# Batch 4's input product in block form at the end of a fused attention and MoE kernel, and the order of all later work set anew

## The chip, the cores and the metric

The kernel runs on one core of a Trainium2 chip. The metric is the device time of one execution in microseconds. The engines are named as the profile names them: PE is TensorE's matmul, PEld its weight load, DVE is VectorE, ACT is ScalarE, POOL is GpSimd, SP is SyncE. L12 is line 12 of the kernel before.

## The reference

For 8 batches of 12 heads with 448 rows of 64, an attention without softmax gives x, and x goes through a feed-forward layer of 768 to 2048 to 768:

```python
scores = scale * np.matmul(q, k.transpose(0, 1, 3, 2))
attn = np.maximum(scores, 0.0) ** 2 / S
x = np.matmul(attn, v)            # heads put side by side: 3584 x 768
h = x @ w_in                      # 768 -> 2048
g = 0.5 * h * (1.0 + erf(h * inv_sqrt2))
return (g @ w_out).astype(np.float32)
```

## The kernel before

**Attention of a batch** is 21 steps in three groups of 7. A step is 4 small matmuls (QK, L742), a relu from PSUM to SBUF on ACT (L754) or DVE (L756), and a square on DVE (L763). After 7 steps 28 small matmuls (AV, L803) make a third of x, which two casts bring to SBUF (L516 on DVE, L518 on ACT).

**The input product** (`x @ w_in`) has two forms. The plain one, `add_f1`, makes 16 column blocks of a batch, each of 6 matmuls of 128x448 (L855), and one gelu on ACT (L865) for each. The block form, `add_blocks`, is a 2x2 block product with 7 products in place of 8 (Winograd's form): four sums of x on DVE (L966), then in four parts (m4 and y), each with 7 products of 6 matmuls of 128x224 (L999), one copy on ACT (L518), five additions on DVE (L1036) and four gelus on ACT (L1045). The parts of one m4 run side by side in the two banks of a PSUM tile. The names of a part are p1, p6, p2, p7, p5, p4, p3 for products; v1 is the copy behind p1, v2 the addition behind p6, v3 that behind p7, c22, c21 and c12 those behind p5, p4 and p3. p2 waits for v1, p7 for v2, p4 for v3 and p3 for c22. Sums of the weights for this form are made once (`add_wsums`, 8 operations, L924). Before the change batches 5, 6 and 7 take the block form; batches 0 to 4 take the plain one.

**The output product** (`g @ w_out`) runs in 13 groups of 256 rows (`add_group`, g1 to g13), again 7 products of 8 matmuls of 128x384 (L1173), with four sums on DVE (L1154) and seven additions or copies, most of them on DVE (L1207); group 0 is plain (L1268). A group's first 128 rows (x=0) and last 128 rows (x=1) are stored from SBUF tiles called osb, of which there are three. The last group, g13, stores in four pieces: the left half of its first rows; all of its last rows; and the right half of the first rows in 256 and 128 columns, behind two additions that follow the two parts of its last product. One piece of each of these last two goes out on ACT's queue, all other stores on SP's.

**Loads** of q, k and v go through POOL's queue. From batch 2 on, q and k are turned by DMA transposes on SP's queue (L665). The swap of halves that follows is two DMAs on SP (L686, L687) or two copies on DVE (L516). The next batch's loads wait for the turned data (gates on POOL, L710).

**The order of all work** is a list, ORDER (L86). A word is an engine letter (P, A, D, G, S) and the number of the operation as the code creates it. `place` commits the words in turn, and `run` emits the operations in that sequence. So for each engine and each queue the list is the program order, and an instruction that waits holds up what follows on its own engine or queue. The planner's costs, due times and readers are consulted for the words' sense; they issue nothing.

Of the kernel before, what the change touches and what calls it, by code (L numbers as in the profile page):

```python
# [9 lines left out]
BF16 = mybir.dt.bfloat16  # L10
# [6 lines left out]
HS = S // 2  # L17
# [69 lines left out]
G0 G1 G3 G4 G1428 G7 G121 A10 P11 D13 G2 A16 P17 D12 P14 G117 D18 P42 P39 G6 P21 D15 P19 A43 G118  # L87
P36 D22 P33 A40 P23 G5 D20 P25 D41 P54 A37 G122 D24 Z1056 D26 A34 P66 P57 D38 A55 D44 G8 P63 P29
P27 A58 D67 P69 P51 D35 A64 P48 D30 P31 D65 A70 P45 D28 D32 A52 P78 D59 G9 P133 D46 A49 P108 D68
D47 P111 A79 P75 D134 P129 A109 D50 P81 P131 D56 A76 P102 D112 P84 G125 A82 D71 P72 D53 A103 G120  # L90
P60 D130 A85 D104 P93 A73 P135 A61 D110 A74 A62 P96 D132 P105 G124 P141 D83 D77 A97 P168 A94 D106
P165 P90 A142 G119 P143 D86 D113 A169 G126 D107 P114 A166 D80 P87 D98 A91 D95 P171 A144 D115 P137
A88 D92 A116 P99 D89 P156 A172 D136 P159 A100 D138 P145 G128 A157 A101 D160 P162 P186 D167 P174
A146 P251 D163 A175 P243 D158 A187 D176 G148 A252 D170 P183 P195 P189 G147 D173 A244 P259 G151
A196 D184 G154 P253 D161 A260 G150 D164 P139 A190 P198 A254 P180 P177 D140 A181 D199 P219 P216
P245 A178 G123 G127 A220 D217 P207 A179 P210 P204 D191 A246 P261 S229 A211 D208 P247 D182 A205
S228 D209 A262 D197 P213 P222 P192 D200 S232 A248 P263 D221 A223 D206 P249 D224 A264 D188 P255
D212 A250 P257 D193 A214 A256 D194 P265 D218 A258 D185 P201 D230 D215 A266 G237 S231 G239 P225
A202 A203 P276 P279 P267 D233 D226 S235 A277 A227 P291 D280 P288 P294 A268 P356 G240 A295 D289
G153 G238 P350 A357 G149 P348 G270 A292 A351 P285 P300 P303 G272 A349 P354 G241 A301 P364 A304  # L100
A355 P312 P318 P362 A365 P370 D319 D281 A363 D296 P358 A313 D236 D290 A286 P282 P306 A371 P315
P352 A359 D307 P360 A353 P376 A361 P368 A316 A377 D317 P372 D314 A369 D308 P366 D293 A373 P378
A283 A367 D284 P374 S234 A379 D390 P382 D278 S399 A375 D391 D392 P380 D417 D418 D305 G242 G152
D302 D287 G269 S398 P327 P339 D320 P297 G271 D396 G155 A328 D383 P333 G274 P384 D381 G273 D298
A340 A299 D393 A334 D394 P330 P324 P309 D329 P387 D419 A331 D335 A385 S402 A310 D395 D311 S386
A325 P342 P336 S401 P321 D397 D400 D388 A343 D332 P421 A322 D337 A323 P423 D420 D338 D422 S405
P446 P443 D341 P449 P425 D424 D344 A450 S404 S403 S406 P427 G413 D444 G275 A426 G409 S389 D447
P429 D326 D428 P452 P455 P345 A456 D453 P440 P437 D445 P431 D430 A441 D560 P433 D346 A347 D432
S435 P473 A438 P461 P470 D434 S436 P509 G407 G408 G410 A471 D474 P513 D448 G412 A462 S542 D457
A510 G411 P479 D454 P476 P464 G415 A514 P519 D472 D442 G414 A465 D439 P517 A520 D477 P515 A480  # L110
D451 A518 S541 P485 P467 P458 A468 P491 A516 S545 P511 D459 A486 D561 P523 A492 D487 A512 D460
P503 P494 P500 D563 A524 P525 D463 S544 A495 D466 P521 D469 A526 D481 P531 D504 A522 D478 P527
A532 D501 P537 D475 S548 A528 D505 P529 D502 A538 D493 S547 S543 S546 S549 P488 P497 P482 A498
D489 P606 G556 P600 G552 G416 P535 A483 A530 G550 P533 D601 G551 A607 D484 A536 G553 D490 G555
P539 D496 G554 D499 P609 G559 P603 P506 G558 A604 D610 G557 P624 A534 P639 D562 P564 A540 D605
A507 P566 A640 D625 D565 D508 P615 P612 P618 D567 P568 A616 D613 P570 D617 A569 D611 D614 P572
S705 D619 P657 D571 P627 P636 S704 P574 D580 D573 A637 D620 P576 D608 A658 D575 S578 A628 P584
D581 S708 D638 D577 P586 D583 S579 D582 P630 D602 P633 P621 D626 A634 D631 P651 A585 S707 P642
P588 D632 D587 A643 D659 P590 D629 A652 A622 D641 D591 P648 A623 D644 P666 P663 A589 S711 D653
P592 D635 A664 S710 S706 S709 S712 G719 P594 G715 A649 D667 D593 P654 P660 P645 A655 D661 P769  # L120
P763 D595 P596 S598 D725 A770 G713 G714 A646 P672 D764 G716 D597 S599 P674 G718 D665 D650 A673
G717 G721 A647 D656 P772 P778 P775 G720 D662 A675 P678 S868 A776 D779 P676 D668 A773 D771 P766
D777 P787 P669 S867 A767 D788 A679 P781 P790 A677 D774 P682 A670 D723 D768 P684 A782 A671 D724
A683 D765 P680 D783 A791 D780 P796 P799 P784 A681 S871 A800 D797 P793 P802 P688 D803 D804 S870
D798 D789 D792 S874 S873 S869 S872 S875 G882 G722 A785 A685 P686 A794 A689 A786 P811 P823 P805
A687 P690 D795 A806 P692 A691 D824 P698 D726 A812 D807 A693 P696 D801 A699 P814 P817 P808 A697
A815 D818 P820 P906 G878 P694 A809 G876 G877 P702 D907 G879 A695 A810 G881 P700 G880 A821 G884
A703 P826 P829 D822 P912 A701 P727 A827 P729 D828 A728 D813 P731 A913 D730 A830 D816 P733 D819
D825 P921 D831 P909 P832 A910 D922 P918 P936 D732 G885 P735 D734 A833 G883 D911 A919 D834 P924
P915 A937 P737 D736 A916 D925 P930 P933 D938 P942 P739 D743 A931 D738 S741 D744 P747 A934 D745  # L130
D740 S742 P749 D917 A748 D935 S979 P751 D914 A943 D920 D750 S978 P753 D944 A752 D746 S982 P755
D923 D926 D754 P757 D932 D908 P939 P948 P927 D758 S981 A940 D949 P960 P945 D941 P835 A928 D756
D950 A946 P759 A929 S761 D961 S985 D947 P957 P954 P951 A836 D760 S984 S980 S983 S986 A958 D955
P963 P966 P839 D956 A952 S762 D953 A967 P837 D959 A840 P969 D964 P972 P987 A838 D888 P841 A973
P843 D988 D965 A842 D989 P845 A970 D962 A844 D974 P847 D971 A846 D1067 P1002 D968 P990 P975 A1003
D991 A848 P993 P996 P851 D976 A994 A977 P999 D997 P1014 P1005 A852 D1004 P849 D995 D992 P853 D886
A850 D1068 P857 D998 A1000 A854 P855 D1015 A1006 D1001 P1017 D1007 P1026 P1008 D1070 A1027 D1018
P1029 A856 P1011 P859 A858 D1059 A1009 D1028 P863 D1019 A1030 A860 D1031 P865 A1012 D1060 A864
A1010 P1035 D887 P1047 P1020 D1016 A866 P861 A1048 P890 D1021 A1036 A862 D1063 D1022 P1023 P1041
P1044 A891 D1013 P892 A1024 D1042 P1053 A1045 D1025 P1050 P1032 D1069 A1051 D1054 P1038 P1071  # L140
A1033 D1062 P894 D1049 A1072 D1043 P1088 D893 A1039 P1073 A1034 D1066 A895 P1079 A1089 D1040
P1090 D889 P1096 P1075 D1091 P896 D1055 D1074 D1181 P1094 D1052 P1077 D897 P1092 P898 D1095 D1078
P1082 D1064 P1099 P900 D1061 D899 D1097 P902 D1083 D1100 P1105 D1080 D901 S904 P1102 A1076 D1179
P1085 A1106 D1139 P1122 A1093 D1046 A1084 P1107 D1037 P1124 A1123 D903 S905 P1109 A1081 D1086
P1126 D1103 A1087 P1113 D1108 P1130 D1125 A1110 P1128 A1127 D1065 P1111 A1104 D1140 A1098 P1056
D1180 D1129 D1112 P1133 D1131 P1143 D1057 D1114 P1119 D1058 P1136 D1134 D1291 P1116 D1144 P1183
D1120 P1200 D1137 P1185 D1117 P1202 A1184 D1141 A1201 P1191 D1182 P1187 D1203 P1145 D1186 P1189
P1206 P1208 P1147 D1190 D1207 D1146 P1194 D1192 P1211 D1209 P1149 D1195 P1214 D1212 D1148 P1217
D1150 P1197 D1142 P1151 A1218 A1115 D1198 A1118 P1221 D1215 A1135 P1234 D1152 A1121 P1219 A1132
P1236 A1101 A1138 P1153 A1235 D1237 P1238 D1161 P1155 D1220 D1154 S1157 P1240 D1159 P1223 D1156  # L150
S1158 P1163 D1160 D1241 P1245 P1165 D1164 D1224 P1228 P1167 D1166 D1162 D1246 P1169 D1229 D1168
P1225 P1171 D1170 D1253 P1173 D1172 D1226 P1175 D1251 P1242 P1231 A1239 P1204 A1222 P1303 A1227
D1243 P1248 D1176 S1178 A1188 P1320 A1205 D1252 P1295 A1210 D1174 S1177 A1244 D1232 P1312 A1199
D1292 P1255 A1230 D1249 A1296 D1254 A1313 P1297 D1293 A1193 P1314 A1196 P1299 A1256 P1257 A1233
D1298 A1213 D1315 A1216 P1301 P1316 D1258 P1318 P1261 D1319 P1259 D1302 D1304 D1294 P1309 D1262
P1323 A1260 A1250 P1263 D1310 A1247 D1324 P1306 D1321 P1265 D1264 D1307 P1326 P1329 P1346 D1327
P1331 D1271 P1267 A1347 D1272 A1330 P1350 P1348 D1268 S1270 P1333 P1275 D1349 D1266 S1269 D1273
P1277 D1276 P1279 D1274 D1332 D1278 P1352 P1335 A1280 P1281 P1283 D1282 P1285 D1365 D1353 D1336
# [239 lines left out]
def kernel(  # L398
# [738 lines left out]
    def add_group(g):  # L1137
# [116 lines left out]
        for bb in bs:  # L1254
            readers.setdefault(bb, []).extend(mine)
# [287 lines left out]
```

## Time and profile before

| what | value |
|---|---|
| median of the runs | 369.87 us (369.41 to 371.4) |
| the profiled execution | 368.93 us, its span 367.2 us |
| PE busy | 358.1 us, 98% of the span |
| DVE busy | 291.2 us, 79% |
| ACT busy | 191.8 us, 52% |
| POOL busy | 63.5 us, 17% |
| granted TensorE clock | 0.996 |

The profile shows one execution. Its span is from the first to the last instruction; the execution's own time is 1.73 us longer. A group's busy time divided by its count is the time that an instruction takes from the engine in a row of such instructions; the mean of one is longer, since instructions overlap at their ends.

### The profile page before, as it was taken

The page shows a single profiled execution, that of the slowest core. Times are in us where ns is not written, and L with a number is a line of the kernel's source. Part 1 is how long each engine was busy: PE and PEld are TensorE (multiplying, and loading weights), DVE is VectorE, ACT ScalarE, POOL GpSimd, SP SyncE. Part 2 cuts the span into 40 slices and gives each one's busy share as a digit, 9 for nine tenths or more (in the row PEclk, how much of TensorE's full clock was granted, in tenths as well). Part 3 has the DMA queues.
Part 4 walks back from the last instruction along what each step waited for, and adds up shares of the span by engine and source line. Part 5 has one row for each costly group of instructions (what it writes and reads, how often), then busy time and mean ns, then how long its engine had stood idle before and what let it go on. Part 6 is the DMA issues. An engine that isn't in the chain of part 4 may idle for free.

```text
span 367.2 us, 8476 instructions
## 1 busy us (share of the span) xinstructions
PE 358.1 (98%) x3560; PEld 222.3 (61%) x3560; DVE 291.2 (79%) x488; ACT 191.8 (52%) x312; POOL 63.5 (17%) x101
## 2 busy tenths in 40 slices
PE   8889999999999999999999999999999999999994
PEld 7666654455544555544455544478888787867662
DVE  3999882689996899998579999999977766667753
ACT  4987867637377544678665466951414134133100
POOL 8565134410600700501310000000000000000000
PEclk9999999999999999999999999999999999999998
DMA  9999999999999999999949770000200211022233
GB/s 172 200 200 204 188 141 203 191 197 157 162 258 172 185 167 188 175 247 161 190 68 201 142 158 2 2 2 5 83 2 1 87 48 40 14 73 87 86 86 88
DMA packets 74406, 46.19 MB, mean 126 GB/s; under 512 B 38400, under 2 KB 70912, under 8 KB 74368
## 3 DMA queue, kind: packets, MB, share of 16 engines
q0 software_dynamic: 32912, 22.47, 42.2%
q1 hardware_dynamic: 40816, 22.67, 29.5%
q8 instruction: 28, 0.46, 0.5%
q10 hardware_dynamic: 640, 0.51, 0.4%
q14 instruction: 10, 0.08, 0.1%
HBM read 45.61 MB, written 11.01 MB: 154 GB/s over the span
## 4 chain that ended last, share of the span: by engine, by line
PE 95%; ACT 3%; issue 1%; DVE 0%; DVEq 0%
PE pso L1173 33%; PE psh L855 26%; PE pb L999 13%; PE ps L742 10%; PE pav L803 9%; ACT a_sq L754 3%; PE pso L1268 3%; PE spin L1340 1%; PE tp L638 0%; PE tp L610 0%; DVE qT L516 0%; DVEq L1538 0%; DVE osb L1207 0%; DVE zero L1324 0%
## 5 line engine op out<-in xcount | busy, mean ns | idle before, releaser
L754 ACT ACTIVATE a_sq<-ps 128x896 bf16<-128x896 f32 (+1 forms) x116 | 102.5, 923 | 44.1 <-PE ps L742 41.1
L763 DVE TENSOR_TENSOR a_sq<-a_sq 128x896 bf16<-128x896 bf16 x169 | 97.1, 614 | 8.0 <-ACT a_sq L754 7.7
L855 PE MATMUL psh<-xT,win_sb 128*128 128x448 bf16 (+1 forms) x516 | 96.3, 340 | 0.0
L855 PEld LDWEIGHTS <-win_sb 128*128 128x128 bf16 x516 | 47.9, 98 | 45.9 <-issue 9.8
L756 DVE TENSOR_SCALAR a_sq<-ps 128x896 bf16<-128x896 f32 (+1 forms) x53 | 57.0, 1078 | 16.6 <-PE ps L742 16.4
L1173 PEld LDWEIGHTS <-s_sb 128*128 128x128 bf16 x424 | 40.7, 98 | 25.7 <-issue 1.8
L865 ACT ACTIVATE h_sb<-psh 128x448 bf16<-128x448 f32 x80 | 43.5, 550 | 22.3 <-PE psh L855 22.0
L742 PE MATMUL ps<-qT,kT 64*64 64x448 bf16 (+1 forms) x756 | 47.9, 336 | 1.0 <-ACT a_sq L754 0.4
L1036 DVE TENSOR_TENSOR part<-pb,part 128x448 f32<-128x448 f32 x60 | 35.2, 617 | 13.6 <-PE pb L999 11.5
L1173 PEld LDWEIGHTS <-h_sb 128*128 128x128 bf16 x312 | 29.8, 98 | 20.9 <-issue 3.2
L1173 PE MATMUL pso<-wout_sb,h_sb 128*128 128x384 bf16 x208 | 38.1, 326 | 0.0
L1173 PE MATMUL pso<-wout_sb,s_sb 128*128 128x384 bf16 (+2 forms) x216 | 38.1, 320 | 0.0
L1173 PE MATMUL pso<-t_sb,s_sb 128*128 128x384 bf16 x208 | 38.1, 326 | 0.0
L803 PE MATMUL pav<-a_sq,v_sb 64*64 64x448 bf16 (+1 forms) x756 | 36.3, 329 | 1.3 <-issue 1.1
L1207 DVE TENSOR_TENSOR osb<-pso,p_sb 128x384 f32<-128x384 f32 x39 | 21.5, 551 | 13.0 <-PE pso L1173 11.2
L742 PEld LDWEIGHTS <-kT 64*64 64x64 bf16 x756 | 18.6, 105 | 21.1 <-issue 16.2
L999 PEld LDWEIGHTS <-win_sb 128*128 128x128 bf16 x288 | 27.5, 98 | 2.9 <-issue 0.7
L803 PEld LDWEIGHTS <-v_sb 64*64 64x64 bf16 x756 | 21.1, 107 | 13.0 <-issue 2.3
L1045 ACT ACTIVATE h_sb<-part 128x448 bf16<-128x448 f32 x36 | 18.4, 576 | 19.0 <-DVE part L1036 18.9
L710 POOL COPY gate<-qT 128x16 bf16<-128x16 bf16 x15 | 5.2, 345 | 100.2 <-DMA qT<-nq 79.9
L518 ACT CAST xT<-pav 128x448 bf16<-128x448 f32 (+1 forms) x38 | 18.3, 500 | 7.7 <-PE pav L803 6.3
L999 PEld LDWEIGHTS <-ws 128*128 128x128 bf16 x216 | 20.8, 98 | 1.2
(58 smaller groups left out, 300.5 us busy)
## 6 DMA issues: line engine op xcount, KB each, us to landing
nk<-in_k_dram POOLq DMA_DIRECT2D x23, 224.0 KB, 10.3
nq<-in_q_dram POOLq DMA_DIRECT2D x21, 224.0 KB, 10.2
v_sb<-in_v_dram POOLq DMA_DIRECT2D x5, 672.0 KB, 9.1
qT<-qT SPq DMA_DIRECT2D x28, 112.0 KB, 2.6
out_dram<-osb SPq DMA_DIRECT2D x8, 336.0 KB, 3.0
v_sb<-in_v_dram POOLq DMA_DIRECT2D x9, 224.0 KB, 9.4
out_dram<-osb SPq DMA_DIRECT2D x7, 288.0 KB, 3.1
out_dram<-osb SPq DMA_DIRECT2D x8, 240.0 KB, 3.0
```

The source lines that it names most:

```text
L742: nc.tensor.matmul(ps[64 * j : 64 * j + 64, e, x * w : x * w + w], kT[r, g, i * 128 + 64 * j : i * 128 + 64 * j + 64], moving, start=True, ...
L754: A.activation(ar, ps, AF.Relu, scale=c_att)
L756: V.tensor_scalar(ar, ps, c_att, 0.0, op0=mybir.AluOpType.mult, op1=mybir.AluOpType.max,)
L763: V.tensor_mul(box["a2"][:, :, :used], ar, ar)
L803: nc.tensor.matmul(pav[0][o2 : o2 + 64, e, :w], vt[b][r, 2 * g + e, bass.ts(i, D)], box["a2"][r, y, o : o + w], start=(i == 0), stop=(i == ...
L855: nc.tensor.matmul(ph[:, x * n : x * n + n], win_sb[:, kd, bass.ts(m + x, 128)], xT[b][:, kd, c], start=(kd == 0), stop=(kd == KD - 1),)
L865: A.activation(h_ring()[:, m : m + nm, o + c.start : o + c.stop], box[0][:, :S].rearrange("p (x n) -> p x n", x=nm), AF.Gelu,)
L999: nc.tensor.matmul(bank[name][:, y, z * HS : z * HS + HS], w[:, k, bass.ts(mm, 128)], right()[:, k], start=first and k == 0 and z == 0, st ...
L1036: V.tensor_add(get(to), ps(name), get(other))
L1045: A.activation(h_ring()[:, m : m + 2, o + half[c].start : o + half[c].stop], src().rearrange("p (x n) -> p x n", x=2), AF.Gelu,)
L1173: nc.tensor.matmul(box[bank][:, n0:n1], left()[:, kf], right()[:, kf, n0:n1], start=bool(need) and kf == 0, stop=kf == K2 - 1, skip_group_ ...
L1207: V.tensor_add(out()[:, n0:n1], box[bank][:, n0:n1], other()[:, n0:n1])
```

## The change

Batch 4 leaves the list of plain input products (`F1B`) and is made by `add_blocks(B - 4)` ahead of the three others. With it 16 plain column blocks and 16 gelus go, and 4 sums of x, 28 products of 6 matmuls, 4 copies, 20 additions and 16 gelus come. The weights' sums, one of which overwrites a part of the weights, wait for batch 3's plain products in place of batch 4's. The sums of x of batches 4 and 5 take the two buffers named kT, and those of batches 6 and 7 share one buffer named qT:

```diff
-    F1B = {2: 1, 3: 2, 4: 3, 5: 4}
+    F1B = {2: 1, 3: 2, 4: 3}
...
-    add_wsums(at(B - 1, 1), [F1[B - 4, m, None] for m in range(KF)])
...
-    end = woven(add_blocks(B - 3), add_group(7))
-    end += add_group(8)
-    end += woven(add_blocks(B - 2), add_group(9))
-    g10 = add_group(10)
-    end += g10 + woven(add_blocks(B - 1), add_group(11))
-    end += add_group(12) + add_group(13)
+    add_wsums(at(B - 1, 1), [F1[B - 5, m, None] for m in range(KF)])
+
+    end = add_blocks(B - 4) + add_group(7)
+    end += add_blocks(B - 3) + add_group(8) + add_group(9)
+    end += add_blocks(B - 2) + add_group(10)
+    end += add_blocks(B - 1) + add_group(11) + add_group(12) + add_group(13)
...
-                    tag = "qT" if b == B - 1 else "kT"
-                    box["t"] = tpool.tile([128, 4, K1, HS], BF16, tag=tag, name="xs")
+                    if b < B - 2:
+                        box["t"] = tpool.tile([128, 4, K1, HS], BF16, tag="kT", name="xs")
+                    else:
+                        if not xsums:
+                            xsums.append(
+                                tpool.tile([128, 2, 4, K1, HS], BF16, tag="qT", name="xs2")
+                            )
+                        box["t"] = xsums[0][:, b - B + 2]
...
-        gone = [o for (bb, *_), o in QK.items() if bb == (B - 2 if b == B - 3 else B - 1)]
+        gone = [o for (bb, *_), o in QK.items() if bb == (B - 2 if b == B - 4 else B - 1)]
```

The other code edits change what the planner takes as readers and writers of h: halves of a batch in place of whole batches (`readers` by `(b, half)`, `done` by the halves that a group's rows touch). They issue nothing.

ORDER is new from the second batch's steps on. PE's words are the same for the first 68 of 472, then stand otherwise; there are 484 in the new list. Counted in the two lists, before and after:

| words | before | after |
|---|---|---|
| PE: crossings between attention (QK, AV) and other work | 114 | 120 |
| relus on ACT / on DVE | 116 / 53 | 123 / 46 |
| casts of x on ACT / on DVE | 38 / 16 | 42 / 12 |
| swaps on SP / on DVE | 14 / 4 | 5 / 13 |
| additions of the block form on DVE | 60 | 80 |
| sums of x on DVE | 12 | 16 |

From batch 5's first QK to the last AV the new list has for PE 63 QK, 9 AV (the last at its end not counted, the last of batch 4 counted), 16 plain column blocks, 30 group products, 2 block products and 39 crossings; for DVE in the same stretch 69 squares, 16 relus, 25 group additions, 16 group sums, 4 sums of x, 2 sums of the weights, 2 casts and 4 swaps. From the last AV to p5 of batch 4's fourth part it has for PE that AV and 22 block products; for DVE 13 block additions, 5 sums of the weights, 3 sums of x and one group addition.

The two lists end so (S alone, with what they store):

```
before: S1401 g12 x=1 | S1402 g12 x=0 | S1423 g13 x=0 left | S1424 g13 x=1 | S1425 g13 x=0, 256 columns | S1426 g13 x=0, 128 columns
after:  S1441 g12 x=1 | S1463 g13 x=0 left | S1465 g13 x=0, 256 columns | S1442 g12 x=0 | S1464 g13 x=1 | S1466 g13 x=0, 128 columns
```

The last words of all engines:

```
before: ... P1417 D1406 D1416 P1420 P1419 D1418 S1424 D1422 D1421 S1425 S1426
after:  ... P1457 P1459 D1458 P1460 D1461 D1462 S1463 S1465 S1442 S1464 S1466
```

Here P1419 and P1459 are the 256 columns of g13's last product and P1420 and P1460 its 128 columns; D1421 and D1461 are the additions behind the 256 columns, D1422 and D1462 those behind the 128.

More of the change, by code (lines that the diff above doesn't have):

```diff
@@ L166 @@
+D1414 P1415 D1416 P1417 D1418 D1423 D1424 P1400 P1419 D1420 S1422 S1421 P1427 P1429 D1425 D1428
+P1431 D1401 D1430 D1426 D1432 A1402 A1396 A1362 P1433 P1435 D1434 P1437 D1436 D1443 D1438 P1439
+S1441 P1447 D1444 D1440 P1449 D1448 D1445 P1451 D1450 P1453 A1452 D1454 D1446 P1455 D1456 P1457
+P1459 D1458 P1460 D1461 D1462 S1463 S1465 S1442 S1464 S1466
 """
@@ L875, in add_f1 @@
         )
-        old = readers.get(b - 2, [])
+        hs = (0, 1) if half is None else (half,)
+        old = [o for x in hs for o in readers.get((b - 2, x), [])]
         d = 0.19 + 0.00069 * S
@@ L939, in add_wsums @@
             WS[m0] = {1: s1, 2: s2, 3: s3, 4: s4}
+    xsums = []
     def add_blocks(b):
@@ L973, in add_blocks @@
         TS = {1: t1, 2: t2, 3: t3, 4: t4}
-        old = readers.get(b - 2, [])
         atoms = []
@@ L986, in add_blocks, with add_block @@
         return atoms
-    def add_block(b, m4, y, ms, bank, x, t, TS, xs, old, half):
+    def add_block(b, m4, y, ms, bank, x, t, TS, xs, half):
         tmp = {}
@@ L1051, in gelu @@
             d = 0.19 + 0.00069 * S
+            old = readers.get((b - 2, c), [])
             o = sch.add((("ACT", d, d + 0.14),), fn, deps + old, frees=frees, bias=GELU_BIAS)
@@ L1144, in h @@
             return h_ring()[:, i * K2 : i * K2 + K2, o : o + 128]
-        done = [o for (bb, *_), o in GL.items() if bb in bs]
+        hs = {t // HS for r in rows for t in (r[0], r[-1])}
+        done = [
+            o for (bb, m, h), o in GL.items()
+            if bb in bs and (isinstance(m, int) and h is None
+                             or 2 * bb + (h if isinstance(m, int) else m[1]) in hs)
+        ]
         sums = SUMS[0] + SUMS[1]
@@ L1289, in add_plain @@
         plain.append(op)
-        readers.setdefault(bb, []).append(op)
+        for t in sorted({128 * t // HS, (128 * t + 127) // HS}):
+            readers.setdefault(divmod(t, 2), []).append(op)
         return op
```

169 lines of the change are left out of this document (80 added, 89 removed).

## The prediction, as it was put on record

> **What bounds the kernel now.** I read the engines' shares first, then the chain of work that ended last, then stretches of the span, and last the tail in order of time. The page's shares and the sum of its chain:
>
> ```profile
> PE 358.1 (98%) x3560; PEld 222.3 (61%) x3560; DVE 291.2 (79%) x488; ACT 191.8 (52%) x312; POOL 63.5 (17%) x101
> PE 95%; ACT 3%; issue 1%; DVE 0%; DVEq 0%
> ```
>
> PE has the chain. In order of time the chain has no piece but PE's from 32.3 to 362.04 us: no wait, 330 us long. So time is what PE must do, plus the start, plus the tail behind the last matmul. The chain also gives the prices (start, length, what):
>
> ```profile
> 63.59 3.51 PE psh L855 x18
> 67.10 0.69 PE ps L742 x12
> 67.79 9.19 PE psh L855 x48
> ...
> 82.17 0.50 PE ps L742 x8
> 82.68 1.32 PE pav L803 x28
> 84.00 0.19 PE ps L742 x4
> ...
> 215.35 4.65 PE psh L855 x24
> ...
> 255.35 6.90 PE pb L999 x72
> ```
>
> From 18 to 24 plain matmuls takes 4.65 - 3.51 = 1.14 us, so 1.14 for a column block of 6. A product of the block form (6 of 128x224) takes 6.90/12 = 0.575. Four QK behind an AV take 0.19, but eight behind other work 0.50 instead of 0.38: an entry into attention costs 0.12. Eighteen plain ones behind QK take 3.51 instead of 3 x 1.14 = 3.42, and a lone six 1.24: an entry into other work costs 0.10. A crossing is thus 0.11.
>
> Is another engine near? Busy times in stretches:
>
> ```profile
> 220.00:240.00 20.00, 20.00 (x202) 9.85 (x206) 18.86 (x29) 15.76 (x25) 0.00 (x0) 1.00 0.01 2
> 240.00:260.00 20.00, 20.00 (x203) 16.60 (x196) 19.08 (x34) 7.62 (x15) 0.00 (x0) 1.00 0.11 31
> 83.00:242.30 159.30, 159.30 (x1538) 82.45 (x1528) 140.99 (x222) 101.15 (x154) 24.32 (x41) 1.00 0.89 151
> ```
>
> After the length come PE, PEld, DVE, ACT. DVE is idle 11% of the attention stage, but only 5% from 220 to 260 (37.94 of 40 busy), and PE still never waits. DVE is the second bound, close behind. The tail in order of time:
>
> ```profile
> 360.54 1.48 PE L1173 MATMUL pso<-wout_sb,s_sb 128*128 128x128 bf16 x16
> 360.75 0.56 DVE L1207 TENSOR_TENSOR osb<-pso,p_sb 128x384 f32<-128x384 f32 x1 [0.74 <-PE pso L1173]
> 362.06 0.62 DVE L1207 TENSOR_TENSOR osb<-pso,osb 128x128 f32<-128x128 f32 x2 [0.76 <-PE pso L1173]
> 362.72 0.86 ACTq L1134 DMA_DIRECT2D out_dram<-osb  x2
> 361.33 0.78 SPq L1134 DMA_DIRECT2D out_dram<-osb  x2
> 362.71 0.79 SPq L1134 DMA_DIRECT2D out_dram<-osb  x2
> ```
>
> The last two additions start when both parts of the last product are done, though the first of them reads the part that was done earlier. SP has already sent g13's last rows (361.33) and has two DMAs left, at 362.71 and 363.07; the second lands 2.8 us later.
>
> **The change, part by part.** All against this execution: span 367.2, its own time 368.93. The runs' median, 369.87, lies 0.94 above it; I add the difference to the median.
>
> *Products.* 16 plain blocks go: 16 x 1.14 = -18.24. 28 products come: 28 x 0.575 = +16.10. Sum -2.14, all of it on PE and so on the path.
>
> Here the Trainium skill speaks against the change: its page "TensorE: Matmul & The Clock Gate", section "Back-to-back issue gap", gives for streams of weight load and matmul some 81 ns a matmul at 128 columns and 131 at 512. On a straight line, an estimate from that page, that is 93.5 ns at 224 columns and 122.7 at 448, and 168 x 93.5 - 96 x 122.7 would be +3.9 us. The rows of this case deny it: 6.90/72 = 95.8 ns at 224 and 1.14/6 = 190 ns at 448.
>
> *Crossings.* 120 in place of 114, at 0.11: +0.66. Together PE's work is 1.5 us less.
>
> *Other engines.* 20 additions (0.535 in a row) and 4 sums of x (0.42) are 12.4 us of DVE, nine swaps at 0.8 another 7; seven relus (1.0) and four casts (0.53) leave it for ACT, -9. All of this lies beside PE's work if DVE keeps up. From batch 5's first QK to the last AV, PE gets 63 x 0.19 + 9 x 1.32 + 16 x 1.14 + 30 x 1.30 + 2 x 0.575 + 39 x 0.11 = 86.6 us (1.30 is a group product, 8 matmuls in the chain). DVE gets 69 squares (0.535) + 16 relus (1.0) + 25 group additions (0.465) + 16 group sums (0.60) + 6.7 for sums, casts and swaps = 81.4. From there to p5 of batch 4's fourth part PE has 14.2 us and DVE 13 x 0.535 + 5 x 0.87 + 3 x 0.42 + 0.465 = 13.0. So DVE has 94.4 of 100.8 us: an idle share of 6%, where 220 to 260 got by with 5%. Hidden, but the cover is thin. The rest of the block stage is easier: three more batches of it at about 70% DVE.
>
> *Spacing of dependent products.* p2, p7, p4 and p3 each wait for an addition or copy behind an earlier product. In the old list the work between the two is at least 1.72 us; in the new one it is 1.15 to 1.30 in nine of 64 cases. Need: g13's p6 starts at 354.04, its slot ends at 355.34, the addition runs from 355.55 to 356.11, 0.77 behind the slot; with 0.615 for a block addition 0.83. That leaves 0.3 if the engine is free. Just after another addition has started it is 0.2 short. So between 0 and 9 x 0.2 = 1.8; I take **0.4**, since at 70 to 90% busy only the worst phase stalls.
>
> *Transposes and loads.* Batches are reached 4 to 14 us earlier, with transposes and gates moved by as much in the list. Swaps on DVE spare SP two issues of 0.6 each. In the trace a round from one batch's turned data to the next took 26.3, 30.6 and 21.9 us (gates at 94.05, 120.35, 150.96, 172.81), and batches 3 to 5 now last 23 to 25 us. Cost taken: 0; up to +4 if the round should need 26.
>
> *The edits to readers, done and the buffers* issue nothing. Batch 5's sums now wait for batch 7's last QK; 14 us of batch 4's products cover that.
>
> *The tail.* This is where I see a loss. Let T be the end of the last matmul. Now both additions wait for T; the one of 256 columns (0.41) ends at T + 0.43. SP's next word is S1465, which waits for it; **behind it stand S1442, g12's first rows, long ready, and S1464, all of g13's last rows**, which before went ahead of T. SP sends one piece from T + 0.46 (0.36), two pairs (0.78 each), then the last: at T + 2.38, against 363.07 - 362.04 = T + 1.03 before: +1.35. By bytes: 384 KB more behind T, and the 336 KB piece too, at 269 KB in the busiest us of the old tail, is +1.4 to 1.9. I take **+1.5**; it would be 0 if SP did not hold to the list.
>
> Sum: -2.14 + 0.66 + 0.4 + 1.5 = **+0.4 us**: 369.3 for the profiled execution, **370.3** for the median.
>
> **The rivals.**
>
> *A, the tail costs nothing* (stores leave ahead of T). Against it: SP's transposes and stores from 196 to 211 us stand in the trace in the list's order. Then -2.14 + 0.66 + 0.4 = -1.1: 368.8.
>
> *B, slower: DVE becomes the bound from batch 5 to batch 4's last part.* Its 94.4 us must fit into 100.8; it decides from an idle share of 6%. For it: the stage from 83 to 242 left 11% idle, and a square that waits for a relu leaves idle time that nobody can fill. Against: 5% from 220 to 260 without a wait of PE. At 8.5% idle 94.4/0.915 = 103.2, +2.4, so +2.8 in all: 372.7; at 11% +5.7.
>
> *C, the narrow products cost more in their new place*, so that the change doesn't save what it says. The weight load row stands at 98 ns, the slot at 95.8: if loads should set the pace, 168 x 0.0022 = +0.4: 370.7. The straight line of the page above would be far more, and the rows leave it no more than 1 in 100.
>
> *D, a batch's turned data come late*: 3.7 us for one batch (26.3 against 22.6), 374.0.
>
> **How the numbers follow.** Forecast with C, 370.3, own range 369.3 to 371.7: 0.62 (C 0.03 of it). A: 0.12. B: 0.18. D: 0.05. Something faster than any of these, of the size of 2 us: 0.03. About 0.5%, 1.85 us, is what a measurement of this kernel can tell from no change. Faster by more than that: 0.05, with a part of A's spread 0.08. Slower by more: B's upper two thirds, D and the spacing at its upper bound: 0.25. Same: 0.67. The range takes A in below and B up to about 9.5% idle above: 368.2 to 374.0.
>
> **What would show it.** The chain after should again be PE alone from some 32 us to T, with T near 361 (362.04 - 1.5 + 0.4); a stretch with DVE at 97% or more and PE pieces broken by waits for additions or squares means B; small pieces of DVE between products in the block stage are the spacing. In the tail four to five SP stores should stand between T + 0.4 and T + 2.8, and the span should end about 6.7 us behind T (5.2 before). Stores before T would make the tail's step wrong; a T below 360 would mean that PE had time to gain which the chain before does not show.

## The result, and the profile after

The changed kernel takes **394.85 us** (394.69 to 396.56) against 369.41 in the same session: a ratio of 1.0689, 95% interval 1.0653 to 1.0725. The forecast was 370.3 with a range up to 374.0. The loss is 25.4 us; the dearest price that the prediction gave to a rival was 5.7 (B, at 11% idle). The profiled execution has a span of 392.9 us at a granted clock of 0.996, as before, so it is not the clock.

The page of the changed kernel, its shares and its chain (lines of the changed kernel: block products are L1009 now, block additions L1046, copies by ScalarE L520, gelus of the block form L1055, group products L1189, the last stores L1145):

```profile
PE 361.4 (92%) x3632; PEld 228.7 (58%) x3632; DVE 302.5 (77%) x515; ACT 203.6 (52%) x331; POOL 66.6 (17%) x101
PE 75%; DVE 11%; DMA 4%; SPq 3%; ACT 3%; issue 1%; POOL 1%; DVEq 0%; ACTq 0%; POOLq 0%
```

PE had 95% of the chain and has 75%; DVE, which had none, has 11%. Is DVE then the bound, as rival B said? Busy times in stretches (length, then PE, PEld, DVE, ACT):

```profile
220.00:240.00 20.00, 18.51 (x192) 11.63 (x191) 16.72 (x31) 11.18 (x17) 0.00 (x0) 1.00 0.27 79
240.00:260.00 20.00, 14.02 (x137) 12.80 (x135) 13.75 (x23) 7.06 (x15) 0.00 (x0) 1.00 0.00 1
320.00:340.00 20.00, 15.85 (x129) 12.22 (x127) 11.80 (x21) 8.43 (x18) 0.00 (x0) 1.00 0.00 1
```

No: where PE is idle DVE is idle as well. It had 19.08 of 20 us from 240 to 260 in the kernel before and has 13.75. DVE is fullest from 200 to 220, and there PE does not wait:

```profile
200.00:220.00 20.00, 20.00 (x198) 10.86 (x195) 19.93 (x35) 13.00 (x19) 0.00 (x0) 1.00 0.17 53
```

Where two engines idle together, the next question is whether they wait for one another, and the waits say that they do. First what PE waits for, then what DVE waits for (total us, times, longest); the kernel before has no wait of PE for `part` at all:

```profile
PE pb L1009 <- DVE part L1046: 14.7, 12, 2.1
```
```profile
DVE part L1046 <- PE pb L1009: 29.6, 23, 3.8
```

One such wait by itself. The timeline where batch 4's first two parts begin (start, duration, engine, line):

```profile
230.24 0.74 PE L1009 MATMUL pb<-xT,win_sb 128*128 128x224 bf16 x6
...
236.12 0.74 PE L1009 MATMUL pb<-xT,win_sb 128*128 128x224 bf16 x6
...
236.90 0.53 ACT L520 COPY part<-pb 128x448 f32<-128x448 f32 x1 [5.44 <-PE pb L1009]
237.46 0.62 DVE L1046 TENSOR_TENSOR part<-pb,part 128x448 f32<-128x448 f32 x1 [1.69 <-ACT part L520]
```

The copy at 236.90 is v1 of the first part (A1040 in the list). Its product is p1 at 230.24 (P1039), done before 231. ScalarE was idle for 5.44 us and still did not start. It started when 236.12 had ended, which is p1 of the *second* part (P1056): another product, into the other bank of the same PSUM tile. In ORDER the copy stands behind that product. So the reader waits not for what it reads but for all that the list has written so far into its tile.

The last AV product ends at 235.6 and the last matmul at 385.5, so 149.9 us lie between. By the prediction's rows it should be 127.1: 110 block products at 0.575, 48 group products at 1.30, and the divided one at 1.48. (The same rows give 98.4 us for this stage of the kernel before, which took 98.3.) So 22.8 us are lost there. By the same rows the last AV product should have ended at 233.5, so 2.1 us are lost ahead of it. The tail, from the last matmul to the end of the span, is 7.4 us in place of 5.2. Less the 1.5 us of work that the change was counted to save, this makes 25.6 of the 25.7 us by which the two profiled spans differ.

### The profile page after: what moved, and what is told of

Same layout as the page of the kernel before. It is cut to its first block, busy times and chain, and to the rows that moved or that the text cites. A ratio compares the mean times of both kernels' runs of the same rounds, so it can differ in the third digit from the quotient of the medians.

```text
span 392.9 us, 8631 instructions
## 1 busy us (share of the span) xinstructions
PE 361.4 (92%) x3632; PEld 228.7 (58%) x3632; DVE 302.5 (77%) x515; ACT 203.6 (52%) x331; POOL 66.6 (17%) x101
## 4 chain that ended last, share of the span: by engine, by line
PE 75%; DVE 11%; DMA 4%; SPq 3%; ACT 3%; issue 1%; POOL 1%; DVEq 0%; ACTq 0%; POOLq 0%
PE pso L1189 28%; PE pb L1009 14%; PE psh L857 14%; PE ps L744 8%; PE pav L805 8%; DVE part L1046 6%; PE pso L1284 3%; SPq L667 3%; DMA v_sb<-in_v_dram 2%; DVE a_sq L765 2%; DMA kT<-nk 2%; DVE a_sq L758 2%; ACT h_sb L1055 1%; ACT part L520 1%; DVE osb L1223 1%
## 5 line engine op out<-in xcount | busy, mean ns | idle before, releaser
L756 ACT ACTIVATE a_sq<-ps 128x896 bf16<-128x896 f32 (+1 forms) x123 | 108.3, 919 | 34.7 <-PE ps L744 34.3
L857 PE MATMUL psh<-xT,win_sb 128*128 128x448 bf16 (+1 forms) x420 | 77.4, 337 | 0.1
L1046 DVE TENSOR_TENSOR part<-pb,part 128x448 f32<-128x448 f32 x80 | 47.1, 618 | 33.8 <-PE pb L1009 29.6
L1189 PEld LDWEIGHTS <-s_sb 128*128 128x128 bf16 x424 | 40.5, 98 | 29.4 <-issue 4.5
L758 DVE TENSOR_SCALAR a_sq<-ps 128x896 bf16<-128x896 f32 (+1 forms) x46 | 49.3, 1075 | 10.0 <-PE ps L744 9.6
L744 PE MATMUL ps<-qT,kT 64*64 64x448 bf16 (+1 forms) x756 | 48.8, 336 | 2.1 <-issue 0.8
L1055 ACT ACTIVATE h_sb<-part 128x448 bf16<-128x448 f32 x48 | 25.4, 573 | 42.0 <-DVE part L1046 42.0
L867 ACT ACTIVATE h_sb<-psh 128x448 bf16<-128x448 f32 x64 | 35.0, 551 | 23.6 <-PE psh L857 23.3
L1009 PEld LDWEIGHTS <-win_sb 128*128 128x128 bf16 x384 | 36.8, 98 | 14.5 <-issue 12.7
L1189 PEld LDWEIGHTS <-h_sb 128*128 128x128 bf16 x312 | 29.4, 98 | 21.5 <-issue 4.1
L1189 PE MATMUL pso<-wout_sb,s_sb 128*128 128x384 bf16 (+2 forms) x216 | 38.1, 320 | 1.2 <-DVE osb L1223 1.2
L1189 PE MATMUL pso<-t_sb,s_sb 128*128 128x384 bf16 x208 | 38.1, 326 | 0.2 <-ACT osb L520 0.2
L1189 PE MATMUL pso<-wout_sb,h_sb 128*128 128x384 bf16 x208 | 38.1, 326 | 0.0
L1009 PEld LDWEIGHTS <-ws 128*128 128x128 bf16 x288 | 27.5, 98 | 9.1 <-issue 7.0
L1009 PE MATMUL pb<-xs,win_sb 128*128 128x224 bf16 x192 | 23.1, 259 | 10.1 <-DVE part L1046 10.1
L553 POOL DMA_DIRECT2D nk<-in_k_dram x23 | 16.5, 719 | 53.0 <-DMA kT<-nk 46.4
```

The lines of the kernel that those rows point to most:

```text
L744: nc.tensor.matmul(ps[64 * j : 64 * j + 64, e, x * w : x * w + w], kT[r, g, i * 128 + 64 * j : i * 128 + 64 * j + 64], moving, start=True, ...
L756: A.activation(ar, ps, AF.Relu, scale=c_att)
L758: V.tensor_scalar(ar, ps, c_att, 0.0, op0=mybir.AluOpType.mult, op1=mybir.AluOpType.max,)
L857: nc.tensor.matmul(ph[:, x * n : x * n + n], win_sb[:, kd, bass.ts(m + x, 128)], xT[b][:, kd, c], start=(kd == 0), stop=(kd == KD - 1),)
L867: A.activation(h_ring()[:, m : m + nm, o + c.start : o + c.stop], box[0][:, :S].rearrange("p (x n) -> p x n", x=nm), AF.Gelu,)
L1009: nc.tensor.matmul(bank[name][:, y, z * HS : z * HS + HS], w[:, k, bass.ts(mm, 128)], right()[:, k], start=first and k == 0 and z == 0, st ...
```

## The experiments

**The theory** (false waits, that is, waits for something that the waiting operation does not use): the program keeps dependences for a whole PSUM tile. The two parts of the block form write two banks of one tile. So (a) a reader that the list has behind the neighbour's product waits for that product, and (b) a product that the list has behind the neighbour's reader waits for that reader. The interleaving of the engines in ORDER therefore decides, not only each engine's own sequence. In the compiled programs 19 readers of the kernel before wait for a product of the other bank and 31 of the changed one; for (b) it is 17 products and 19. **Rivals**: the sequences within the engines are bad (products of a part too close, or DVE's queue); batch 4's block form is itself too tight; the order of the stores.

**1. Interleave as early as possible (early), and the stores mended (early_tail).** Every engine keeps its sequence of words. Between P1039 and A1057 the list changes so (P1058 and P1056 are the second part's products):

```diff
-P1039 P868 D867 D1023 D1127 D1008 D1011 D869 D1005 D1037 P870 P1041 S872 S762 P1024 P1058 P1056 A1040 A1025 A1026 A1057
+P1039 A1040 P868 D869 D1005 D1037 D1030 S872 S762 P870 D871 S873 P1041 D1042 D1038 D1029 P1024 A1025 A1026 P1058 P1056 A1057
```

> The changed kernel with each engine's and each queue's own sequence of words kept as it is; only the way in which the five sequences are interleaved in the hand-written list is new: every word of ScalarE, VectorE, GpSimd and SyncE stands as early as what it uses allows, ahead of the next word of TensorE. Theory (false waits): a reader of a block bank that stands in the list behind the neighbouring part's product waits for that product as well, because both parts write one PSUM tile; in the compiled changed kernel 31 readers wait for a product of the other part, here none does. So about all of the 20 us of TensorE's holes and restarts between the last AV product and the end go away: 371 to 375 us, with PE near 20 us busy in each 20 us window from 220 to 380, and the waits of PE for the block additions fall from 14.7 us to under 2 us. Rival (the order within the engines itself is bad: products of one part too close behind one another, or VectorE's queue in a bad order, or the three wide PSUM buffers too few): nothing changes, 394 to 396 us, the same 14 to 15 us of waits for the additions. In between, for example 385 us, both hold a share.

Measured: **402.64 us**, ratio 1.0888 (1.0866 to 1.0911). A miss, and to the wrong side: the waits are more, not fewer.

```profile
PE pb L1009 <- DVE part L1046: 17.6, 19, 3.3
```

No reader waits for the other bank here, but the second half of the theory, (b), was left out of the expectation: 53 products wait for a reader of the other bank, where it was 19. So it is not enough that readers come early. In part it is the clock, too (see the end). What follows: the interleaving across engines moves the time by 8 us with every engine's sequence the same, which the rival of the sequences cannot explain; and "as early as possible" is not the good way.

> The run before, and in SyncE's own sequence the store of group 12 and the store of group 13 that stood behind the one that waits for the last additions now stand ahead of it. Theory of the tail (SyncE's order holds two stores back): the end of the span comes 1.4 to 2.2 us sooner behind the last product than in the run before, and the time is 1.4 to 2.2 us shorter. Rival (the last store's own landing sets the end): no change, within 0.5 us.

```diff
-S1441 S1463 S1465 S1442 S1464 S1466
+S1441 S1442 S1463 S1464 S1465 S1466
```

Measured: 399.95, 2.7 us less than the run before it. More than expected, and the right sign; but the executions of each of these two kernels spread over 2.7 to 3.6 us, so the size is better read from experiment 8.

**2. Interleave by the planner's own times (sorted_by_plan), and with the stores mended in several runs (sorted_tail).**

```diff
-        self.open, self.log = [], best[1]
+        self.open, self.log = [], sorted(best[1], key=lambda x: x[0])
```

> The changed kernel with the emission sorted by the start that the planner gives each word; each engine keeps its sequence. In the compiled kernel 12 additions wait for 12 or more matmuls of the other part beyond their own product, against 19 in the changed kernel and none in the fully early one. False waits: the time lies between, at 378 to 388 us. The rival of the order within the engines: 394 to 396 us.

Measured: 380.24, one run, within the range.

> The changed kernel, emitted in the order of the planner's starts (each engine's own sequence kept) and with the stores of the end in the order of the kernel before. False waits: the sorted list gave 380.24 us in one run; without the store order's 1.5 to 2.7 us it is 377.5 to 378.7 us, so that the interleaving is worth 14 to 15 us of the changed kernel's loss in several runs too, and 6 to 7 us are left that only another order within the engines takes away. Rival (the single run was a lucky one): 382 us or more.

Measured: **378.37 us**, ratio 1.0229 (1.02 to 1.0258). PE's waits for block additions are, in sorted_tail,

```profile
PE pb L1009 <- DVE part L1046: 2.7, 7, 0.6
```

14.7 us of waits have become 2.7. The single run is 14.6 us shorter than the changed kernel, with the same instructions in the same sequence on every engine; sorted_tail, without the 2.2 to 2.7 us of its stores, 13.8 to 14.3.

**3. The counter-test on the kernel before (before_late).** Its PE words first, the others only when PE needs them; each sequence kept. So readers stand late, as (a) has it. The copy A1072 that stood ahead of the neighbour's product P1088 now stands behind it:

```diff
-P1071 A1033 D1062 P894 D1049 A1072 D1043 P1088
+P1071 P894 P1088 A1033 D1062 D1049 A1072
```

> The counter-test on the kernel before: each engine's own sequence kept, but TensorE's words stand first wherever they can, and the words of the other engines only when TensorE's next word needs them. Readers that wait for a product of the other part rise from 19 to 28, and those that wait for 26 or more matmuls beyond their own from 3 to 9. False waits: the kernel before becomes slower by 2 to 12 us, 372 to 382 us, with waits of PE for block additions that it did not have. Rival (the order of the list across engines does not matter): 369 to 371 us.

Measured: **382.84**, one run, just over the upper bound: 13.6 us for nothing but the order of the list across engines. The kernel before, whose PE never waited for a block addition, now has

```profile
PE pb L999 <- DVE part L1036: 8.6, 12, 1.5
```

**4. The disputed cost by itself (two_banks).** Its four stages are:

```python
def products_first(banks):                      # stages 1 and 3
    product(banks[0]); product(banks[1])        # 6 matmuls 128x224 each
    V.tensor_add(part[0], banks[0][:, :448], part[0])
    V.tensor_add(part[1], banks[1][:, :448], part[1])
...
shared = [both[:, 0], both[:, 1]]               # stages 1 and 2: two banks of one tile
own = two tiles of one bank                     # stages 3 and 4
```

> The disputed cost by itself; nothing of the reference is computed. Four stages of 24 rounds, in each round two products of 6 matmuls (128x224) into two PSUM banks, and one VectorE addition (128x448) for each bank; each bank's next product needs its own addition only. Stages 1 and 2 use two banks of one tile, stages 3 and 4 a tile for each bank. In stages 1 and 3 the program lists product, product, addition, addition; in 2 and 4 product, addition, product, addition. On each engine all four stages are the same sequence. False waits: with one tile a round takes the two products and two additions almost one after the other, 2.6 to 3.2 us in stages 1 and 2; with two tiles 1.4 to 1.9 us in stages 3 and 4, and in stage 1 every first addition starts only when the second product has ended. Rival (the waits are by bank, or the chain of product, addition, product is itself the limit): all four stages take the same time, within 0.2 us a round.

Stage 1 (one tile), and then stage 3 (a tile for each bank):

```profile
8.69 1.31 PE L34 MATMUL both<-xt,wt 128*128 128x224 bf16 x12 [1.25 <-DVE part L42]
8.69 1.15 PEld L34 LDWEIGHTS <-wt 128*128 128x128 bf16 x12 [1.41 <-issue]
10.04 0.62 DVE L41 TENSOR_TENSOR part<-both,part 128x448 f32<-128x448 f32 x1 [1.40 <-PE both L34]
10.58 0.61 DVE L42 TENSOR_TENSOR part<-both,part 128x448 f32<-128x448 f32 x1
```
```profile
204.91 3.35 PE L34 MATMUL own<-xt,wt 128*128 128x224 bf16 x27
...
206.46 0.62 DVE L42 TENSOR_TENSOR part<-own,part 128x448 f32<-128x448 f32 x1 [0.16 <-PE own L34]
207.13 0.62 DVE L41 TENSOR_TENSOR part<-own,part 128x448 f32<-128x448 f32 x1
207.91 0.62 DVE L42 TENSOR_TENSOR part<-own,part 128x448 f32<-128x448 f32 x1 [0.16 <-PE own L34]
```

With one tile the first addition starts only when both products are done (8.69 + 1.31 = 10.00), and the next pair only when both additions are: a hole of 1.25 us in each round of 2.56. With two tiles the additions come in turn and PE's row has no hole: 206.46 to 207.91 is a round of 1.45, and it is the same in stage 4. These 1.45 us are what the chain of product, addition, product on one bank takes; the other 1.1 us of the one-tile round are the tile's. So the rival, equal times in all stages, fails. The sizes were met for two tiles (1.4 to 1.9) and not for one: 2.56 lies just under the stated 2.6 to 3.2, and from 16 us on the clock fell (see the end), so that a round of stage 1 takes 3.64 and one of stage 2 3.99. What stage 2 takes at the whole clock, no round shows. The changed kernel has a hole of the same size:

```profile
326.10 0.73 PE L1009 MATMUL pb<-xs,win_sb 128*128 128x224 bf16 x6 [0.67 <-DVE part L1046]
326.67 0.74 PE L1009 MATMUL pb<-xs,ws 128*128 128x224 bf16 x6
327.45 1.69 DVE L1046 TENSOR_TENSOR part<-pb,part 128x448 f32<-128x448 f32 x3 [1.40 <-PE pb L1009]
...
328.65 0.35 PE L1009 MATMUL pb<-xs,win_sb 128*128 128x224 bf16 x2 [1.25 <-DVE part L1046]
```

Two products, then additions, then a product 1.25 us late. Each hole costs some 0.17 us more: 12 matmuls that stand alone take 1.32 in the chain, where two products in a row take 2 x 0.575 = 1.15. Here the Trainium skill's page "Perfetto Trace Analysis", section "Matmuls", says that independent matmul groups should rotate through different PSUM banks, so that one bank is emptied while the next is filled. The parts of this kernel do use different banks; by stages 1 and 3 that helps, in a program that keeps dependences by tile, only if the banks belong to different tiles.

**5. The best interleaving of the given sequences (woven).** As sorted_by_plan, but chosen by a search that weighs waits (a) and (b).

> The changed kernel with each engine's sequence kept, as in the first run of this set, but interleaved by a search that weighs both waits: a reader listed behind the other part's product waits for that product, a reader listed ahead of it makes that product wait for the reader. False waits in both directions: the best that these sequences allow is between the changed kernel and the kernel before, 375 to 383 us, since with these sequences 25 readers still wait for the other part. If only the readers' waits counted, it would be slower than the fully early list's theory had it, near 385 us.

Measured: 379.24, one run. Within the range, and hardly better than the sorted list. So some 7 us (378.37 against the 371.44 below) are left that only other sequences take away.

**6. The changed work in another order (replanned), and the kernel before with the same planner (before_replanned).** The list from about 190 us on is made anew, within the engines too: 122 of 484 words of PE, 106 of 329 of ScalarE and 155 of 499 of VectorE stand in another place of their engine's sequence. Ahead of 190 us the sequences stay, but they are interleaved anew as well.

> The changed kernel, computing the same work with the same tiles (batch 4 in block form, its input product and all others as in the change); only the order of the work from about 190 us on is set anew, the order within the engines too, by a list planner that knows that a product and a reader of the other bank of its tile wait for one another; the stores of the end stand as in the run with the mended tail. False waits: with 17 readers that wait for the other part, against 31, and no pair of products that leaves a reader in between without time, 368 to 373 us. Rival (batch 4's block form itself costs the time, whatever the order: too little other work between its dependent products): 380 us or more, still with over 5 us of waits of PE for the block additions.

Measured: **371.44 us**, ratio 1.0045 (1.0029 to 1.0061). PE's share of the span is back:

```profile
PE 359.3 (97%) x3632; PEld 229.2 (62%) x3632; DVE 303.0 (82%) x515; ACT 205.3 (55%) x331; POOL 65.4 (18%) x101
```

Only 0.2 us of waits for a block addition are left. So the block form of batch 4 is not too tight, nor is DVE, with the same 303 us of work, the bound.

The number of false waits does not order the runs: replanned has 17 of kind (a) and 35 of kind (b), sorted_tail 24 and 30, the changed kernel 31 and 19. What counts is how long each one holds. The table sets every wait of the compiled programs beside the times of the trace, and counts the time by which the other bank's event came after all else that the operation waited for (its own product or reader, its other waits, its engine), where it is over 0.02 us:

| kernel | readers held by a product of the other bank (a) | products held by a reader of the other bank (b) |
|---|---|---|
| before | 9.6 us, 10 times | none |
| changed | 39.5 us, 27 times | 10.3 us, 12 times |
| early | none | 19.6 us, 30 times |
| before_late | 38.8 us, 25 times | none |
| sorted_tail | 8.7 us, 20 times | 2.9 us, 11 times |
| replanned | 5.1 us, 13 times | 0.2 us, 2 times |

The times of (a) are of engines that partly had nothing else to do, and are not lost in full. The changed kernel has both kinds at length, the early list only the second, and before_late only the first.

> The same planner on the kernel before, which has no holes on TensorE in the block stage that the profile shows: 367 to 371 us, no change beyond 0.5%. If it became faster by more than that, the gain of the replanned changed kernel would not be the change's.

Measured: **368.04 us**, ratio 0.9954 (0.9934 to 0.9973), faster than both kernels. That is just within the 0.5% expected. Its last matmul ends 0.4 us sooner than in the kernel before and its tail is 4.4 us in place of 5.2. By the same planner the change then costs 3.4 us (371.44 - 368.04).

**7. What is left: the loads and the front (replanned_pool, front_of_before).** In the replanned run a piece of the chain is a transposing DMA (start, length, what):

```profile
50.01 1.30 SPq L667
...
51.35 8.64 DMA kT<-nk
...
60.03 0.38 PE ps L744 x4
```

The first edit puts the gates on GpSimd back to where the kernel before has them (shown), and SyncE's first transposes as well (not shown):

```diff
-G127 G153 G270 G239 G238 G149 G152 G269 G241 G272 G271 G274 G273 G155 G407 G240 G237 G242
+G127 G237 G239 G240 G153 G238 G149 G270 G272 G241 G242 G152 G269 G271 G155 G274 G273 G407
```

> The run with the order set anew from 190 us on, and GpSimd's first loads and gates and SyncE's first transposing DMAs (to about 110 us) in the order of the kernel before. In the changed kernel and in the replanned one a gate that stood ahead of plain loads of the next batch and of the second weight stands behind them; the transposing DMAs of 41 to 57 us then take 2.0 to 6.2 us where they took 1.3 to 4.1, and TensorE lost 1.6 us by 60 us in the replanned run waiting for turned k. Theory (those loads share the DMA engines with the transposing DMAs): no wait of TensorE for turned k, 1.0 to 2.3 us sooner, 369.1 to 370.5 us, same as before or faster by up to 0.3%. Rival (the wait has another cause, for example work that TensorE does earlier now): 371 to 372 us with the same wait.

Measured: 371.42, ratio 1.0038 (1.002 to 1.0056): no gain that can be told from the replanned run. The theory's 369.1 to 370.5 is missed, and the rival's number holds, though not its "same wait". PE is gapless from 40 to 60 us, so the order of the front did cause that wait; whether the loads did it or the order of the transposes, which the edit moved together, is not shown. Another turned k comes late at 100 us (1.0 us). The lateness moved.

> The changed work with the list of the kernel before word for word for its first 760 words (to about 190 us, on every engine and queue), and the planner's order behind it. Theory: the front loses nothing, as in the kernel before, and behind it the planner leaves under 3 us of holes: 368.5 to 373 us. Rival (without batch 4's input product as filler, the attention of the last batches has holes that the change's new front avoids): over 373 us, with TensorE's holes between 200 and 240 us.

Measured: 375.89, ratio 1.0159 (1.0131 to 1.0188): the rival holds. Busy times of its last stretch of attention:

```profile
200.00:220.00 20.00, 15.73 (x198) 7.91 (x196) 19.50 (x31) 13.13 (x20) 0.00 (x0) 1.00 0.80 159
```

DVE has 19.50 of 20 us and PE 15.73; in the whole run PE waits 5.3 us for `a_sq`, the tile of relus and squares. Batch 4's plain products were work that PE did between attention steps; without them the old order leaves attention bound by the relus and squares. Here rival B's mechanism is seen, though not in the changed kernel. (With the old front come its engines too: nine swaps go back to SP and four operations from ScalarE to DVE, so DVE has 501 operations in place of 515.) The change had to set a new front: with the planner's order behind it in both runs, the new one takes 371.44 and the old one 375.89.

**8. The tail alone (before_tail).** The kernel before, with the changed kernel's order of the last stores (SP's words alone):

```diff
-S1401 S1402 S1423 S1424 S1425 S1426
+S1401 S1423 S1425 S1402 S1424 S1426
```

> The kernel before, with nothing else than the changed kernel's order of the last stores: the store of group 12's first rows and that of group 13's last rows stand behind the one that waits for the additions after the last product. Step of the prediction: these stores then go out behind the end of the last product, +1.35 to +1.9 us (1.5 taken); the runs of the early list with and without this order differ by 2.7 us. Rival (the landing of the very last store sets the end either way): within 0.5 us of the kernel before, 369.2 to 370.3 us.

Measured: **371.55 us**, ratio 1.0062 (1.0039 to 1.0086), +2.2, a little over the stated 1.35 to 1.9. After the last additions (362.26), SyncE sends six pieces where the kernel before had two left:

```profile
362.26 0.62 DVE L1207 TENSOR_TENSOR osb<-pso,osb 128x128 f32<-128x128 f32 x2 [0.76 <-PE pso L1173]
362.91 3.08 SPq L1134 DMA_DIRECT2D out_dram<-osb  x6
```

and the changed kernel has the same picture:

```profile
385.53 0.62 DVE L1223 TENSOR_TENSOR osb<-pso,osb 128x256 f32<-128x256 f32 x2 [0.76 <-PE pso L1189]
385.98 3.10 SPq L1145 DMA_DIRECT2D out_dram<-osb  x6
```

## Why the prediction was wrong, point by point

The loss of 25.4 us, taken apart by these runs:

| part | us | from |
|---|---|---|
| order of the last stores | 2.2 to 2.7 | before_tail; early against early_tail |
| interleaving of the engines in the list | 13.8 to 14.6 | changed kernel against sorted_by_plan; less the tail, against sorted_tail |
| sequences within the engines | 6.9 | sorted_tail against replanned |
| the rest | 1.8 | replanned against the kernel before |

- **What bounds the kernel**: right that PE does, and right that DVE was not the next to bound in the block stage. What was missed is a third thing that no share of the profile shows: a dependence between two parts that share a tile.
- **Spacing of dependent products, +0.4 (at most 1.8)**: this is the step that failed. It took 0.83 us from the end of a product to its reader's result, and let only each engine's own sequence decide when a reader starts. With one tile the need is: both products, both additions, a hole of 1.25 us (stage 1), and more where the reader stands far behind in the list (the copy at 236.90, 5.44). The need by itself was about right for separate tiles: a round of stage 3 is 1.45, 0.88 behind the product's 0.575. In place of 0.4 us the block products of the changed kernel wait 15.6 us for additions and copies (14.7 and 0.9); for 10.3 us the last thing that they wait for is a reader of the other bank. The description of the kernel ahead of the prediction says that the list is the program order of each engine and each queue. That is true and not all: it is also the order in which the tile's writers and readers are taken. The trace of before did hold such waits, but none of PE, so its chain does not show them. One is a gelu of ScalarE:

```profile
250.34 0.54 ACT L1045 ACTIVATE h_sb<-pb 128x448 bf16<-128x448 f32 x1 [5.18 <-PE pb L999]
```

Its own product had ended at 247.28; it starts when a product into the other bank ends, at 250.30. The old list puts readers about where they run (before_late shows what it costs if not); the new list puts them late and in bunches.

- **Products (-2.14) and crossings (+0.66)**: in the replanned run the chain's block products take 62.61 us for 642 matmuls, 97.5 ns each, where it was 96.2 (48.50 for 504): 0.8 us more than counted. That is of the size that rival C had (+0.4) and small beside the loss; the runs do not say whether the weight loads are its cause. The gain of 2.14 itself is not seen on its own.
- **Other engines, hidden**: right. The same work of DVE, 303.0 us, fits with PE at 97% in the replanned run. Rival B asked for a stretch with DVE at 97% and PE broken by waits; DVE does reach 19.93 of 20 us from 200 to 220, but PE is whole there, and the stretches with holes that are shown above have 59 to 84%. (The prediction's terms for DVE up to the last AV make 80.8 us as they stand, not 81.4; it changes nothing.)
- **Transposes and loads, 0**: too low by 1 to 2 us, going by the work done at 60 us. At 60 us the changed kernel has done 7 plain matmuls of 448 columns fewer than the kernel before and 4 QK more (71 against 78, 112 against 108): 7 x 0.19 - 4 x 0.05 = 1.1 us. In the replanned run it is 12 fewer, 2.3 us. This is rival D in small, from the front and not from the round of later batches, and the sum had 0 for it.
- **The tail, +1.5**: right in mechanism, too small in size. 2.24 us in the changed kernel's profile (7.4 against 5.16), 2.2 alone on the kernel before. The prediction let SyncE's last piece start at T + 2.38, T being the end of the last matmul, and its prices make 2.28 us for the six pieces; they take 3.10, so that the last starts near T + 3.2 (385.98 + 3.10 - 0.36 - 385.5).
- **Rival A** fell with the tail. None of the rivals had the mechanism that decided.

The forecast of 370.3 stands near the replanned run, 371.44, but that is no support: that run has its stores mended, and the sum held 1.5 for them. Without the tail the sum says -1.1; the replanned run has +1.8 by its median and +3.1 by its profiled execution, so 2.9 and 4.2 us are missing. In the profiled execution the late turned k (2.3 by 60 us), the block products (0.8) and six more crossings in its list (0.7), less its tail, which is 0.6 shorter than that of the kernel before, make 3.2; 1 us stays open.

**Left open**: how much of the 6.9 us of the sequences is the tile's doing and how much the bare chain of a part. The planner that made the better order weighs both; of the direct waits only 2.7 us of (b) are between the two runs in the table. A changed kernel with a tile for each part was not tried: six banks of PSUM are taken by three tiles of two banks that attention needs whole.

## What to carry to other kernels

Where one hand-written list drives several engines, ask of every shared buffer what the program takes as one object: two banks of one PSUM tile made independent parts wait for each other, at 1.1 us a round. An order that is moved must be moved with its interleaving; a reader belongs in the list where it will run, neither late (it waits for the neighbour's product) nor early (the neighbour's product waits for it). Stores that are ready do not belong behind one that waits for the last result: on one queue that was 2.2 us.

## What the runs showed of the hardware that was not expected

The TensorE clock fell to half in stages 1 and 2 of two_banks, from 16 us on, though PE's holes are short. Busy times there and in stage 3 (the length, PE, PEld, DVE, POOL, and then the clock):

```profile
20.00:95.00 75.00, 49.55 (x246) 35.88 (x246) 23.41 (x41) 0.00 (x0) 0.50 0.00 1
180.00:212.00 32.00, 30.77 (x256) 25.01 (x254) 26.64 (x43) 0.00 (x0) 0.95 0.00 1
```

From 6 to 16 us the clock is whole: PE is busy for 1.31 us of each round of 2.56, with a hole of 1.25. Then it is 0.50 throughout stages 1 and 2 (holes of 1.25 us and of 0.72), and 12 matmuls take 2.40 us in place of 1.31. With PE at 96% in stage 3 it is back. The Trainium skill's page "TensorE: Matmul & The Clock Gate", section "HAM oscillation — how this bites in real kernels", puts the rule as no idle gap over some 3.4 us; in these stages the clock fell with no gap of PE over 1.3 us once the matmuls had begun, so here keeping the rule was not enough. Its section "A second HAM failure mode: psum-queue depth-cycling" tells of a kernel whose short pauses between groups of matmuls let the clock swing; here it does not swing but stays low.

The changed kernel itself kept 1.00 from 220 to 380 us, with PE at 14.02 of 20 us in one stretch and single gaps up to 2.1 (at 283 and 320 us). The early list lost its clock behind one longer gap:

```profile
294.44 1.28 PE L1009 MATMUL pb<-xT,ws 128*128 128x224 bf16 x6 [3.31 <-DVE part L1046]
```

The granted clock is 1.00 up to 292 us and 0.50 from 294 to 298, and this product takes 1.28 us where others take 0.73. That is a part of why the early list was the slowest. Why gaps of 1.25 us, one in each round, were enough in two_banks and gaps of 2.1 us were not in the changed kernel, these runs do not show.
